# Moving the last-stage chunks of the inverse transform to a block's first step, and holding back one output product in fewer places

## The chip, the cores and the metric

One core of one Trainium2 chip runs the whole program. The time is the device time of one execution in microseconds. Of three timed runs of the kernel before, the median is 2562.79 us (2562.3 to 2563.24). All other times are from one profiled execution, which took 2563.68 us by the same clock; its trace spans 2561.9 us. Instructions stand under their engines: PE (matrix), DVE (vector), ACT (scalar), POOL (GpSimd) and SP, which issues most DMAs.

## What is computed

```
x: (8, 3008, 256)   filt_r, filt_i: (1505, 256)   w_in: (256, 2048)   w_out: (2048, 256)
y = irfft(rfft(x, axis=1) * (filt_r + 1j * filt_i), n=3008, axis=1)
t = y.reshape(24064, 256)
h = t @ w_in
out = (h * clip(h + 3, 0, 6) / 6) @ w_out
```

All of it is in fp32. So there is a circular convolution along the sequence, for eight batches, and behind it a two-layer network with the hardswish function between the layers, for 24064 tokens.

## The kernel before

**Blocks and steps.** The network works on 47 blocks of 512 tokens (256 pairs of tokens). A block has eight steps, one for each 256 of the 2048 hidden features. One pass of the main loop (L1442 on) does the first layer ("up") of step p and the second layer ("down") of the step before it. Both layers are written as seven products of quarter size in place of eight (a Strassen form). The seven up products are in `up_1` (three of them), `up_2` (two), `up_3` and `up_5` (one each); they add up in the two PSUM tiles `al` and `be`. The seven down products are called by number, `down(k, p, 1)` and so on, and add up over the eight steps of a block in four PSUM tiles `po0` to `po3`. In the order of PE, a step without anything special is: up_1, down 1, up_2, down 2 and 4, up_3, down 5 and 6, up_5, down 7 and 3. The down products always belong to the step before.

**What the other engines do in a step.** ACT copies partial sums out of `al` and `be` (L966, L967, L976, L995) and computes the inner clip (`relu`, L1000). DVE adds up the hidden values (L981, L986), multiplies (`hswish`, L1005, twice a step), and makes the sums that the down products need: `g_sums` with L1012 and L1013, and `g_last` with L1018, which product 3 needs. L1005, L1012, L1013 and L1018 read two operands from SBUF; L981, L986 and the output lines read one of theirs from PSUM.

**The turn of a block.** The down products of step 7 of a block run in step 0 of the next. Then the block's result is taken out of `po0` to `po3`: `out_1` (ACT, L1089) behind products 2 and 4 of step 0; `out_2` and `out_3` (DVE, L1098 and L1103) at the end of step 0; `out_4` (DVE, L1107 and L1108, both reading `po2`; POOL, L1109) and `out_5` (DVE, L1112) in step 1. The first product of a new block that writes `po2` is number 5, in step 1. It has to wait until L1108 has read the old value.

**The transform.** While the blocks of one batch run, the transform of the next batches is made in pieces, called from a table `plan`: `plan[step, place]` lists functions, and the loop calls `do(place)` at fixed points of a step. Place 0 is behind `up_1`, place 1 ahead of the first `hswish`, place 2 at the step's end, and places 3 and 4 at its head. The pieces that matter here:

- `n_five` (L881), a last-stage chunk: 40 products of PE (L892, 80 matmul rows in the trace) make 235 pairs of tokens from five rows; ACT copies them to the ring `xn` (L872); when a block's input is complete, `ready` calls `t_sums` (L940): seven POOL additions (L947) that make `xt` from `xn`, both operands from SBUF.
- "Units" (`a8_unit` L608, `b8_unit` L706, `bi8_unit` L779): 16 products in 32 matmul rows that write `al`, `be` and two more PSUM tiles. They stand at place 3, so at the head of a step, ahead of its `up_1`.
- `half_sums`, `a8_folds` (DVE, L522 and L626) and `z8_store` (DMAs from POOL's and SP's queues, L647 and L650): from the second stage to the first of a batch's transform.

Blocks have a kind: for each batch from the third on, the blocks seven to two before its first block are `c a x F F F`; the rest are `t`. `FIVE_AT` (L1311) gives, by kind, the step within a block in which a chunk of five rows is put: three numbers, for a block with one chunk and for the first and second of two. In the kernel before most chunks of `a`, `x` and `F` blocks stand in step 1, place 0.

**Held product.** Where the next step has a unit at its head, the loop leaves product 3 out at the step's end (`held`, L1525) and issues it behind the unit, ahead of products 1 and 2 of the next step, which in such a step also come ahead of `up_1`:

```python
            if units:
                do(3)
                if held:
                    down(*held, 3)
                g_sums(kd, pd)
...
                held = (kd, pd) if (i + 1, 3) in plan and pd < NP - 1 else None
                down(kd, pd, *((7,) if held else (7, 3)))
```

The program has 63 such units, all held.

Of the kernel before, what the change touches and what calls it, by code (L numbers as in the profile page):

```python
# [53 lines left out]
NP = DFF // 256  # L54
# [175 lines left out]
def kernel(  # L230
# [602 lines left out]
    def pair(i):  # L833
        b, js, o, n = chunks[i]
        return b * HC * NA + o, n
# [118 lines left out]
    def product(ps, p, w, x, start=False, stop=False):  # L954
        strips(ps, w_in[p][:, w, :], x, start=start, stop=stop)
# [14 lines left out]
    def up_2(k, p):  # L970
        t = st["xt", k]
        al, be, s, s5 = st["up"]
        h = [hp.tile([P, 512], FP32, name="h%d" % i) for i in range(2)]
        product(al, p, S2, t[:, F3, :])
        product(be[:, 1, :], p, S4, t[:, F5, :], stop=True)
        nc.scalar.activation(out=s[:, 1, :], in_=al, func=AXT.Copy)  # L976
        st["h"] = h
# [10 lines left out]
    def up_4(k, p):  # L988
        st["g", k, p] = gp.tile([P, 7, 256], FP32, name="g")
        relu(0)  # L990
# [46 lines left out]
    def last_down():  # L1037
        p, v, add = NP - 1, nc.vector.tensor_tensor, ALU.add
        g, o = st["g", LAST, p], st["o", LAST][0]
        hswish(LAST, p, 1)  # L1040
        ps = [psF.tile([P, 512], FP32, name="psf", tag="f") for t in range(2)]
        for i, a in ((0, G11), (1, G12)):
            for t in range(2):
                for u in range(2):
                    strips(ps[t][:, ts(u, D)], g[:, a + t, ts(u, P)], w_out[p][:, 2 * i:2 * i + 2, :].rearrange("p j m -> p (j m)"),
                           start=i == 0 and u == 0, stop=i == 1)
        out_4(LAST)
        v(out=o_at(LAST, 0, 1), in0=st["po", LAST][3][:, 1, :, :], in1=o_at(LAST, 0, 1), op=add)
        for t, qs in ((0, (nc.sync, nc.scalar)), (1, (nc.sync, nc.scalar))):
            both = o[:, t, :, :].rearrange("p u d -> p (u d)")  # L1050
            v(out=both, in0=ps[t], in1=both, op=add)
            store_last(t, qs)
# [6 lines left out]
    def plain_up(p):  # L1059
        st["g", 0, p] = gp.tile([P, 7, 256], FP32, name="g")  # L1060
        st["h"] = [psU.tile([P, 512], FP32, name=n) for n in ("al", "be")]
        for i in range(2):
            for d in range(2):
                strips(st["h"][i], w_in[p][:, 2 * d + i, :], xn[:, d, :, 0:PAIRS], start=d == 0, stop=d == 1)
            relu(i)
            hswish(0, p, i)

    def plain_down(p, tokens=(0, 1)):
        g = st["g", 0, p]
        if p == 0:  # L1070
            st["po", 0] = [psO.tile([P, 2, 2, P], FP32, name="po%d" % i) for i in range(2)]
        for t in tokens:
            for u in range(2):
                for i, a in ((0, G11), (1, G12)):
                    strips(st["po", 0][t][:, u, :, :].rearrange("p a m -> p (a m)"), g[:, a + t, ts(u, P)],
                           w_out[p][:, 2 * i:2 * i + 2, :].rearrange("p j m -> p (j m)"),
                           start=p == 0 and u == 0 and i == 0, stop=p == NP - 1)
# [81 lines left out]
    plan = {}  # L1159
# [4 lines left out]
    def at(step, fn, *a):  # L1164
        plan.setdefault((step, 0 if fn in EARLY else 1 if fn is w_scale else 2), []).append((fn, a))

    with tc.manual_schedule():
# [140 lines left out]
                kinds[first[n] - 7 + d] = kind  # L1308

        N_AT = {"c": ((6, 6), (1, 1), (6, 6)), "F": ((0, 0), (1, 1), (6, 6)), "t": ((2, 4), (2, 4), (6, 6))}  # L1310
        FIVE_AT = {"c": (6, 3, 6), "a": (1, 1, 5), "x": (1, 1, 5), "F": (1, 0, 1), "t": (4, 2, 4)}  # L1311
        N_FIRST = {0: ((3, 4),), 1: ((), (2, 2), (3, 3)), 2: ((1, 1),), 3: ((1, 1),)}
        in_block = {}
        for i in range(2, len(chunks)):
# [2 lines left out]
        for i in range(2, len(chunks)):  # L1317
            k = pair(i)[0] // PAIRS
            head = chunks[i][2] == 0
            same = in_block[k]  # L1320
            at_, kind = same.index(i) + 1 if len(same) > 1 else 0, kinds.get(k - 1, "t")
            steps = N_FIRST[k - 1][at_] if k - 1 in N_FIRST else (FIVE_AT[kind][at_],) * 2 if len(chunks[i][1]) == NJ else N_AT[kind][at_]
            if head and len(same) == 1:
                steps = (6, 6)
            s0, s1 = ((k - 1) * NP + s for s in steps)
            five = len(chunks[i][1]) == NJ
            n_at[i] = s1
            if head:
                stored = s0 - 3 + (k == first[1])
            at(max(stored, n_at[i - 2] + 1), t4_load, i)  # L1330
            if five:
                at(s1, n_five, i)
                continue
            at(s0, n_unit, i, 0)
            at(s1, n_unit, i, 1)
# [8 lines left out]
        ZERO_AT = ((6, 1), (6, 1), (7, 0), (7, 1), (8, 0))  # L1344
        ZERO2_AT = ((9, 0), (9, 0), (9, 1), (10, 0), (10, 0))
        A2_AT = (5, 11, 18, 21)
        SUM2_AT = ((0, 1), (3, 4), (10, 14), (15, 16))
        FOLD2_AT = ((7, 8), (12, 13), (19, 20), (22, 23))
        LOAD2_AT = (-4, -2, 5, 11)

        def places(n):
# [23 lines left out]
        for n in range(1, B):  # L1375
# [7 lines left out]
            for c, s in enumerate(a_at):  # L1383
# [7 lines left out]
                k = (first[n] - 7) * NP  # L1391
                sums, folds, load = (SUM2_AT, FOLD2_AT, LOAD2_AT) if n == 2 else (SUM_AT, FOLD_AT, LOAD_AT)
                for d in range(2):
# [46 lines left out]
        held = None  # L1440
        items = [(k, p) for k in range(NBLK) for p in range(NP)]
        for i in range(len(items) + 1):  # L1442
            up = i < len(items)
            k, p = items[min(i, len(items) - 1)]
            dn = i > 0
            kd, pd = items[i - 1]
            def do(place):
                for fn, a in plan.get((i, place), ()):
                    fn(*a)

            if k == 0:
                plain_up(p)
                do(0)
                if dn:
                    plain_down(pd)
                do(1)
                do(2)
                continue
            if not up:
                last_down()  # L1460
                break
            ends = k == LAST and p == NP - 1
            last_plain = dn and kd == 0
            dn = dn and kd > 0
            units = [fn for fn, a in plan.get((i, 3), ())]
            inverse = bool(units)
            ahead = (1, 2) if inverse else (1,) if units else ()
# [5 lines that stand above are left out]
                if not late(i):  # L1473
                    g_last(kd, pd)
                do(4)
                down(kd, pd, *ahead)
                up_1(k, p)
                do(0)
                down(kd, pd, 4 if inverse else 2)
            else:  # L1480
                up_1(k, p)
                do(0)
                if dn:
                    g_sums(kd, pd)
                    if not late(i):
                        g_last(kd, pd)
                    down(kd, pd, 1)
            if up:
                up_2(k, p)
            if dn and pd == 0 and kd > 1:  # L1490
                out_4(kd - 1)
            if up:
                up_2b(k, p)
            if dn:
                down(kd, pd, *((5,) if inverse else (4,) if units else (2, 4)), us=(0,) if inverse else (0, 1))
                if pd == NP - 1:
                    out_1(kd)
            if up:
                up_3(k, p)
                if dn and late(i) and not (pd == 0 and kd > 1):  # L1500
                    g_last(kd, pd)
            if dn:
                down(kd, pd, 5, us=(1,) if inverse else (0, 1))
                down(kd, pd, 6)
            if up:
                up_4(k, p)
            if ends:
                out_1(k)
            if last_plain:
                plain_down(pd, (0,))  # L1510
            if dn and pd == 0 and kd > 1:
                out_5(kd - 1)
                g_last(kd, pd)
            if up:
                do(1)
                hswish(k, p, 0)
            if up:
                up_5(k, p)
            if last_plain:
                plain_down(pd, (1,))  # L1520
                plain_out()
            if dn:
                if pd == NP - 1 or ends:
                    out_2(kd)
                held = (kd, pd) if (i + 1, 3) in plan and pd < NP - 1 else None  # L1525
                down(kd, pd, *((7,) if held else (7, 3)))
                if pd == NP - 1 or ends:
                    out_3(kd)
            do(2)
# [30 lines left out]
```

## Time and profile before

| quantity | value |
|---|---|
| timed runs, median (lowest to highest) | 2562.79 us (2562.3 to 2563.24) |
| profiled execution, its own time | 2563.68 us |
| its span in the trace | 2561.9 us |
| granted PE clock | 1.00 of full speed over the span |
| POOL L947 (`t_sums`), time of one | 727 ns median for `xt<-xn`, 792 ns for `xt<-xt` |
| DVE L1005 (`hswish`), time of one | 746 ns mean of 736 |

How to read it: PE matmuls are pipelined, and a matmul's row lasts until its modelled end, so the rows of successive groups overlap. What counts on PE is the time from the start of one group to the start of the next. The same holds for a step: its length is the time from the first `al<-xt` group of its `up_1` to that of the next step. A row of the timeline is: start in us from the span's start, duration in us, engine, line, operation, output and input tiles, shape, count, and in brackets the idle time before it with what ended it.

### The profile page before, as it was taken

The numbers are of one execution on the slowest core, as the hardware profiler recorded it, in microseconds if no ns is written. First come the engines' busy times: TensorE is split into PE (matmuls) and PEld (weight loads), VectorE is DVE, ScalarE is ACT, GpSimd is POOL, SyncE is SP. The second block draws the span as 40 slices with busy tenths as digits, with TensorE's granted clock in tenths as the row PEclk, the third lists the DMA queues.
The fourth block names the chain that finished last, engine by engine and source line by source line (L and its number), as shares of the span: only waits on it lengthen the run. The fifth ranks groups of instructions, "written<-read, shape, count | busy, mean of one in ns | idle before, by whom it ended". The sixth has DMA issues, their size and how long they took to land.

```text
span 2561.9 us, 87054 instructions
## 1 busy us (share of the span) xinstructions
PE 2542.2 (99%) x37890; PEld 2011.1 (79%) x37890; DVE 2076.5 (81%) x3645; ACT 1321.4 (52%) x2716; POOL 458.7 (18%) x648
## 2 busy tenths in 40 slices
PE   8999999999999999999999999999999999999998
PEld 4488787877888788877887878887788877888887
DVE  6977888888888888888888888888888888766666
ACT  4554455555555555555555555555555555555554
POOL 3252021120211202112021110212102121011110
PEclk9999999999999999999999999999999999999999
DMA  8845545422333133232332323323222232111000
GB/s 234 236 120 164 158 119 153 146 94 86 104 102 115 55 90 110 88 116 59 97 109 80 114 61 105 100 89 105 85 56 63 71 95 71 42 45 26 19 22 26
DMA packets 178180, 245.43 MB, mean 96 GB/s; under 512 B 21354, under 2 KB 143752, under 8 KB 177414
## 3 DMA queue, kind: packets, MB, share of 16 engines
q1 hardware_dynamic: 163997, 200.76, 26.7%
q0 software_dynamic: 13472, 38.81, 5.3%
q8 instruction: 297, 4.87, 0.8%
q14 instruction: 85, 0.70, 0.1%
q10 hardware_dynamic: 329, 0.30, 0.0%
HBM read 164.38 MB, written 128.81 MB: 114 GB/s over the span
## 4 chain that ended last, share of the span: by engine, by line
PE 96%; DVE 1%; DMA 1%; ACT 0%; issue 0%; SPq 0%; DVEq 0%; ACTq 0%
PE po L952 45%; PE al L952 25%; PE be L952 19%; PE psn L892 2%; PE al L779 1%; PE be L608 1%; PE psf L706 1%; DMA bits<-in_moe_w_in_dram 0%; PE psf L693 0%; PE psf L589 0%; ACT h L995 0%; DMA w_all<-in_x_dram 0%; PE psf L763 0%; PE al L608 0%; PE psn L952 0%
## 5 line engine op out<-in xcount | busy, mean ns | idle before, releaser
L952 PEld LDWEIGHTS po<-w_all,g 128*64 128x64 f32 x20808 | 1235.7, 137 | 277.3 <-DVE g L1005 29.4
L952 PE MATMUL po<-w_all,g 128*64 128x128 f32 (+1 forms) x20808 | 1422.6, 275 | 1.9 <-DVE o L1108 1.0
L1000 ACT ACTIVATE r<-h,half_c 128x512 f32<-128x512 f32 x736 | 531.0, 722 | 302.4 <-DVE h L981 290.2
L952 PE MATMUL al<-xt,w_all 128*64 128x256 f32 x4416 | 667.7, 381 | 0.1
L1005 DVE SCALAR_TENSOR_TENSOR g<-r,h 128x512 f32<-128x512 f32 x736 | 546.6, 746 | 95.7 <-ACT r L1000 86.2
L952 PE MATMUL be<-xt,w_all 128*64 128x256 f32 x2944 | 442.9, 379 | 0.0
L981 DVE TENSOR_TENSOR h<-be,s 128x512 f32<-128x512 f32 x368 | 254.1, 690 | 169.1 <-PE be L952 138.2
L995 ACT ACTIVATE h<-al 128x256 f32<-128x256 f32 x368 | 141.0, 383 | 302.1 <-PE al L952 298.1
L952 PEld LDWEIGHTS be<-xt,w_all 128*64 128x64 f32 x2944 | 211.9, 137 | 105.8
L952 PEld LDWEIGHTS al<-xt,w_all 128*64 128x64 f32 x4416 | 275.9, 137 | 6.0 <-POOL w_all L469 1.0
L986 DVE TENSOR_TENSOR h<-al,s 128x256 f32<-128x256 f32 x368 | 156.2, 424 | 150.1 <-PE al L952 150.1
L1013 DVE TENSOR_TENSOR g<-g 128x512 f32<-128x512 f32 x367 | 267.1, 728 | 12.6
L947 POOL TENSOR_TENSOR xt<-xn 128x256 f32<-128x256 f32 x184 | 147.1, 817 | 697.6 <-ACT xn L872 697.6
L952 PE MATMUL al<-xn,w_all 128*64 128x256 f32 (+1 forms) x1536 | 240.1, 392 | 1.0 <-DVE g L1005 0.6
L952 PE MATMUL be<-xn,w_all 128*64 128x256 f32 (+1 forms) x1536 | 236.5, 388 | 0.0
L967 ACT ACTIVATE s<-be 128x256 f32<-128x256 f32 x368 | 141.0, 383 | 176.0 <-PE be L952 176.0
L976 ACT ACTIVATE s<-al 128x256 f32<-128x256 f32 x368 | 141.3, 384 | 160.7 <-PE al L952 160.5
L966 ACT ACTIVATE s<-al 128x256 f32<-128x256 f32 x368 | 141.6, 385 | 102.0 <-PE al L952 102.0
L1012 DVE TENSOR_TENSOR g<-g 128x256 f32<-128x256 f32 x367 | 174.1, 474 | 12.6
L1018 DVE TENSOR_TENSOR g<-g 128x256 f32<-128x256 f32 x367 | 168.0, 458 | 1.5
L796 POOL DMA_DIRECT2D g_tmp<-t x84 | 44.8, 540 | 663.8 <-DVE t L790 663.8
L952 PEld LDWEIGHTS be<-xn,w_all 128*64 128x64 f32 x1536 | 110.5, 137 | 62.0 <-issue 7.4
(192 smaller groups left out, 1887.6 us busy)
## 6 DMA issues: line engine op xcount, KB each, us to landing
g_tmp<-t POOLq DMA_DIRECT2D x96, 256.0 KB, 4.4
x_tmp<-in_x_dram SPq DMA_DIRECT2D x54, 384.0 KB
t<-g_tmp SPq DMA_DIRECT2D x168, 120.0 KB
ft<-f_tmp SPq DMA_DIRECT2D x36, 512.0 KB
t<-zp_tmp SPq DMA_DIRECT2D x36, 512.0 KB
o_tmp<-o SPq DMA_DIRECT2D x46, 256.0 KB
zp_tmp<-y POOLq DMA_DIRECT2D x96, 96.0 KB, 4.3
zp_tmp<-y SPq DMA_DIRECT2D x84, 96.0 KB
```

The costliest lines, as they stand in the source:

```text
L947: nc.gpsimd.tensor_tensor(out=o, in0=x0, in1=x1, op=op_)
L952: nc.tensor.matmul(ps[ds(o, STRIP)], w[:, ds(o, STRIP)], x, skip_group_check=True, **kw)
L966: nc.scalar.activation(out=s[:, 0, :], in_=al, func=AXT.Copy)
L967: nc.scalar.activation(out=s5, in_=be[:, 1, :], func=AXT.Copy)
L976: nc.scalar.activation(out=s[:, 1, :], in_=al, func=AXT.Copy)
L981: nc.vector.tensor_tensor(out=st["h"][0].rearrange("p (a n) -> p a n", a=2), in0=be, in1=s, op=ALU.add)
L986: nc.vector.tensor_tensor(out=st["h"][1][:, 256:512], in0=al, in1=s5, op=ALU.add)
L1000: nc.scalar.activation(out=r, in_=st["h"][i], func=AXT.Relu, bias=half_c, scale=1.0 / 6.0)
L1005: nc.vector.scalar_tensor_tensor(out=st["g", k, p][:, o:o + 2, :].rearrange("p a n -> p (a n)"), in0=st["r", i], scalar=1.0, in1=st["h"][i ...
L1012: v.tensor_tensor(out=g[:, G1, :], in0=g[:, G3, :], in1=g[:, G22, :], op=ALU.add)
L1013: v.tensor_tensor(out=g[:, G3:G2 + 1:2, :], in0=g[:, G3:G1 + 1, :], in1=g[:, G11:G11 + 1, :].broadcast_to([P, 2, 256]), op=ALU.subtract)
L1018: nc.vector.tensor_tensor(out=g[:, G4, :], in0=g[:, G12, :], in1=g[:, G2, :], op=ALU.subtract)
```

## The change

```diff
-        FIVE_AT = {"c": (6, 3, 6), "a": (1, 1, 5), "x": (1, 1, 5), "F": (1, 0, 1), "t": (4, 2, 4)}
+        FIVE_AT = {"c": (6, 3, 6), "a": (0, 0, 5), "x": (1, 1, 5), "F": (0, 0, 1), "t": (4, 2, 4)}
...
-                at(s1, n_five, i)
+                plan.setdefault((s1, 5 if kind in "aF" and at_ < 2 and s1 % NP == 0 else 0), []).append((n_five, (i,)))
...
-        SUM2_AT = ((0, 1), (3, 4), (10, 14), (15, 16))
-        FOLD2_AT = ((7, 8), (12, 13), (19, 20), (22, 23))
+        SUM2_AT = ((0, 1), (3, 4), (10, 12), (15, 16))
+        FOLD2_AT = ((7, 8), (13, 14), (19, 20), (22, 23))
...
             if up:
                 up_2(k, p)
+                do(5)
...
-                held = (kd, pd) if (i + 1, 3) in plan and pd < NP - 1 else None
+                held = (kd, pd) if (i + 1, 3) in plan and any(fn is n_five for fn, a in plan.get((i, 0), ())) else None
```

There are three parts.

1. In blocks of the kinds `a` and `F`, a chunk goes to step 0, at a new place 5 between `up_2` and products 2 and 4. That moves 20 chunks from step 1: one in each of 6 `a` blocks and 14 `F` blocks, each of them followed by a `t_sums`. Two more chunks, in blocks 32 and 37, were in step 0 already, at place 0, and go to place 5; those have no `t_sums`. The DMAs that load a later chunk's input (`t4_load`) are issued one step earlier with them.
2. Product 3 is held back only where the step itself has a chunk at place 0. That leaves 8 of the 63 cases: the `x` blocks and step 1 of blocks 32 and 37.
3. For the third batch, the second pair of `a8_folds` goes from steps 12 and 13 behind that batch's `c` block's start to 13 and 14, and a `half_sums` from 14 to 12.

No instruction is added or taken away.

## Prediction

> **What bounds the kernel now.** First the page's busy times and its chain of what ended last: PE.
>
> ```profile
> span 2561.9 us, 87054 instructions
> PE 2542.2 (99%) x37890; PEld 2011.1 (79%) x37890; DVE 2076.5 (81%) x3645; ACT 1321.4 (52%) x2716; POOL 458.7 (18%) x648
> PE 96%; DVE 1%; DMA 1%; ACT 0%; issue 0%; SPq 0%; DVEq 0%; ACTq 0%
> ```
>
> As no matmul is added or removed, time can only come or go where PE stands still. Those places are few, so the step lengths are next, from the timeline of PE (first `al<-xt` group to first `al<-xt` group). A plain step is 6.08 us. A chunk adds 1.46 (step 0 of block 32: 7.54). A step with a unit behind it is 8.30, and the step after the unit 5.35 (products 1 and 2 went ahead). So a step with a chunk and a unit should be 8.30 + 1.46 = 9.76. The windows of block 27, steps 0 to 2, show 9.95, and those of blocks 33 and 34, steps 0 and 1, show something else:
>
> ```profile
> 1513.17:1519.24 6.07, 6.07 (x88) 5.06 (x86) 5.25 (x10) 3.45 (x8) 2.12 (x4) 1.00 0.57 148
> 1519.24:1529.19 9.95, 9.95 (x217) 7.45 (x214) 8.04 (x14) 5.57 (x11) 5.78 (x7) 1.00 0.06 19
> 1529.19:1534.54 5.35, 5.35 (x72) 4.15 (x70) 5.00 (x9) 2.49 (x6) 0.90 (x2) 1.00 0.25 68
> 1831.69:1838.42 6.73, 6.73 (x104) 5.73 (x102) 5.36 (x9) 4.12 (x12) 5.23 (x9) 1.00 0.58 153
> 1838.42:1847.34 8.92, 8.57 (x137) 6.12 (x135) 8.02 (x16) 4.55 (x9) 3.35 (x4) 1.00 0.14 43
> ```
>
> (Columns: window and length, then busy time of PE, weight loads, DVE, ACT, POOL, with instructions.) Block 33 has no `n_five`, but a short chunk in step 0 with a `t_sums` behind it. Its step 1 should be 8.30 and is 8.92. This is the row the prediction rests on, so here is that stretch on DVE, POOL and PE:
>
> ```profile
> 1836.80 0.76 DVE L1018 TENSOR_TENSOR g<-g 128x256 f32<-128x256 f32 x1
> 1837.48 1.22 DVE L1005 SCALAR_TENSOR_TENSOR g<-r,h 128x512 f32<-128x512 f32 x1
> 1838.62 0.68 DVE L1098 TENSOR_TENSOR o<-po,p 128x512 f32<-128x512 f32 x1
> ...
> 1840.56 0.83 DVE L1012 TENSOR_TENSOR g<-g 128x256 f32<-128x256 f32 x1
> 1841.43 0.69 DVE L1013 TENSOR_TENSOR g<-g 128x512 f32<-128x512 f32 x1
> 1842.04 0.42 DVE L1107 TENSOR_TENSOR o<-po,o 128x256 f32<-128x256 f32 x1
> 1842.37 0.41 DVE L1108 TENSOR_TENSOR o<-po,o 128x256 f32<-128x256 f32 x1
> ```
>
> ```profile
> 1835.15 2.11 POOL L947 TENSOR_TENSOR xt<-xn 128x256 f32<-128x256 f32 x3
> 1837.35 1.95 POOL L947 TENSOR_TENSOR xt<-xt 128x256 f32<-128x256 f32 x2
> 1840.06 1.05 POOL L947 TENSOR_TENSOR xt<-xt 128x256 f32<-128x256 f32 x1
> ```
>
> ```profile
> 1841.89 0.60 PE L952 MATMUL al<-xt,w_all 128*64 128x256 f32 x4
> 1842.84 1.09 PE L952 MATMUL po<-w_all,g 128*64 128x128 f32 x16 [0.35 <-DVE o L1108]
> ```
>
> DVE's additions with two SBUF operands are slow while `t_sums` runs on POOL (L1018 0.76 for 0.41, L1005 1.22 for 0.69, L1012 0.83 for 0.43); those with a PSUM operand are not (L1098 0.68). So L1108 ends 1842.78, and product 5, which writes `po2`, starts 1842.84, where 1841.89 + 0.43 = 1842.32 was due: 0.52 us lost, and 0.10 more in the re-start of the next groups. In block 34, with no chunk, L1108 ends 3.18 us behind the step's start and nothing waits: product 5 is due at 3.90, so DVE has 0.7 us to spare there.
>
> **Part 1, chunks to step 0.** The chunk's own 1.46 us go along unchanged: ahead of it stands `be<-xt` and behind it `po`, as now. What goes: in step 1 of today's 19 such blocks with a unit behind (9.75 to 9.98 us against 9.76), products 1 and 2 wait after the unit for DVE, delayed by `t_sums`; the excess adds up to 3.0 us. Without `t_sums` there, block 33 shows no such wait after its unit. What comes: `t_sums` falls on the turn of the block. Its place follows from rows. In step 0 (plain plan: up_1 1.30, down 1 0.44, up_2 0.86, re-start 0.10) the chunk starts at 2.70. In block 27 `t_sums` starts 2.53 behind the chunk's start (chunk 1520.64, POOL 1523.17). So it starts at 5.23 of a step of 7.54: 2.31 before step 1. In block 33 it started 3.27 before step 1 and ended 2.7 behind it. Everything else in step 0 from product 2 on (p14, L986, relu, L1005, L1098) shifts by the same 1.46 as step 1 does, so DVE's order and dates against step 1 are those of block 33. There `t_sums` caught L1018, the first L1005, a little of the second (0.78) and L1012, and missed L1013. Coming 0.96 later it catches up to all of the second L1005 (1.21, +0.43) and of L1013 (1.10 in block 27, +0.41). The lost time per block is thus between 0.62 (as in block 33) and 0.62 + 0.84 = 1.46. I take half of the extra, **1.04**, as seven additions that last some 6 us from -2.31 end at about 3.7, which catches part of both. For 19 blocks: 19.8 us.
>
> The Trainium skill (SBUF — State Buffer, Who interferes with whom) says that a DVE instruction with two SBUF inputs contends with a GpSimd instruction that reads SBUF, and that the one that comes second is fully blocked till the other ends. The rows agree on which instructions suffer; a wholly overlapped L1005 takes 1.21 and not 0.69 + 0.73.
>
> The 20th block is 5, the third batch's `a` block. There two `a8_folds` (L626, two SBUF operands) stand between L1103 and the second L1005, so L1108 ended 4.39 behind step 1's start even without `t_sums`; only the chunk in step 1 covered that. Uncovered it is 0.5 late; with the 0.8 that L1018 and the first L1005 add, and up to 0.5 each for the two folds and the second L1005, the loss is 1.3 to 2.8. I take 2.6, less the 0.2 lost there now: **+2.4**.
>
> Moves that cost nothing: the `t4_load`s of these chunks were issued at least 17.1 us ahead of their chunk, which now comes some 5 us earlier; the two chunks from place 0 to place 5 have no `t_sums`, and step 0 has no wait. In `a` blocks `z8_store` now stands behind `t_sums` in POOL's queue, some 9 us later, but the next pair of folds that needs its buffer comes over 20 us behind. `out_4`'s POOL addition gets earlier.
>
> **Part 2, holding back.** PE's work between up_5 and product 2 is the same either way; product 3 only changes sides with the unit. 55 cases change. Product 3 needs L1018, which in block 33 ends 1844.37, and product 3 would be due there at 1844.69. The other side: ACT's two copies out of a unit's `al` and `be` end 0.83 and 1.32 behind the unit, and up_1 would write those tiles 0.92 and 1.35 behind it. Nothing, up to 0.02 x 55 = 1.1 us. On the gain side, `bi8_unit` waits for ACT's copy of `al` (waits: 6.0 us of weight loads, 21 times), but its steps are 8.303 us against 8.297 of `a8_unit`, which doesn't wait: 0.1 us in all. **0**.
>
> **Part 3, the folds.** In block 5 the second L626 of the pair stands still for 2.17 us for a store from its buffer, and PE behind it:
>
> ```profile
> 382.82 0.69 DVE L626 TENSOR_TENSOR y<-t 128x512 f32<-128x512 f32 x1
> 385.67 0.69 DVE L626 TENSOR_TENSOR y<-t 128x512 f32<-128x512 f32 x1 [2.17 <-DMA zp_tmp<-y]
> ```
>
> That step is 7.05 us for 6.08. One step later the store is long done, and the `half_sums` (L522, 1.22) that takes its place delays nobody in step 6 of that block, where it stands now: **-0.97**.
>
> **Sum.** 19.8 - 3.0 + 2.4 + 0 - 0.97 = +18.2 us on the profiled execution's 2563.68, so 2581.9; the median is 0.9 below that execution, so **2581.0**, 0.7% slower. Its own range: all blocks at 0.62, block 5 at +1.1: +8.9, so 2571.7; all at 1.46, block 5 at +2.6, and the 1.1 of part 2: 27.7 - 3.0 + 2.6 - 1.0 + 1.1 = +27.4, so 2590.2.
>
> **Rivals.**
> 1. The wait for `po2` does not form. Then only gains are left: -3.0 - 0.2 - 0.97 = -4.2, so 2558.6. It decides at L1108: if it ends by 3.85 of step 1, product 5 is on time. For it speaks the 0.7 us of spare in block 34 and that DVE is idle for 2 us in step 0 during the chunk. Against it: that idle time comes before L986, so it can't be used, and blocks 33 and 39 (8.92, 8.90) both show the wait under an earlier, milder overlap. A partial wait of up to 0.4 a block ends near here too. **Chance 0.11**.
> 2. The held product is what makes `bi8_unit` late: its first matmul comes 0.319 behind the last `po`, against 0.202 for the other units, and if that 0.117 is truly lost, product 3 ahead of the unit saves it 21 times, 2.5 us. On top of rival 1 that is 2556.1, **faster** by 0.26%. It decides at L1108 as 1 does, and by bi8's steps falling below 8.25. Against it: the unit's other matmuls come closer together, so that those steps are as long as a8's. **Chance 0.06**.
> 3. Each SBUF addition of DVE waits for a whole POOL addition (0.73), so that L1018, both L1005, L1012 and L1013 each grow by that. L1108 then ends near 5.9, 2.1 lost a block: 39.9 - 3.0 + 2.6 - 1.0 = +38.5, 2601.3. Read strictly, this is the rule of the page above. The 92 wholly overlapped L1005 rows are against it. **Chance 0.04**.
>
> **How the numbers follow.** The forecast has 0.79. Changes within 0.2% (5.1 us) are what a measurement of this kernel hardly tells from none. Slower: 0.79 + 0.04 = 0.83; same: 0.11; faster: 0.06. The range goes from 2566 (a loss of some 0.3 us a block, below block 33's row) to 2591; left out are the two faster rivals (0.17), and the far end of the third, as near to 2 in 10 as the cases allow.
>
> **What would show it.** In the profile after, step 0 of the `a` and `F` blocks should be 7.54; step 1 8.30 + about 1.0, with the gap between up_3 and product 5 and L1108 as its releaser; L947 rows from 2.3 us before step 1 to 3.7 into it, and the second L1005 and L1013 longer than 0.69. The steps with a unit and no chunk should stay at 8.30. Block 5's step 5 should be 6.08, its step 1 above 8. The prediction is wrong if L1108 ends before 3.9 in those steps, or if up_1 begins to wait for ACT's copies behind the units.

## The result and the profile after

The changed kernel takes 2583.26 us (median of 6 runs, 2582.04 to 2586.59), the kernel before beside it 2562.05 us (6 runs, 2561.29 to 2563.24). The ratio is 1.0085, with a 95% interval of 1.0072 to 1.0098: slower by 0.85%, where 2581.0 us and 0.7% were forecast. The profiled execution took 2582.13 us, at a granted clock of 1.00 as before.

From the page of the kernel after, the span, the busy times and the chain that ended last:

```profile
span 2580.3 us, 87055 instructions
PE 2543.8 (99%) x37890; PEld 1998.2 (77%) x37890; DVE 2067.0 (80%) x3645; ACT 1321.8 (51%) x2716; POOL 463.0 (18%) x648
PE 94%; DVE 4%; issue 1%; ACT 0%; DMA 0%; SPq 0%; DVEq 0%; ACTq 0%
```

DVE's share of the chain goes from 1% to 4%, although DVE is busy for no longer than before: it works as much and is waited for more. The waits of PE say for what (total us, times, longest):

```profile
PE po L952 <- DVE o L1108: 16.3, 23, 1.1
PE po L952 <- DVE g L1005: 3.4, 3, 2.0
```

The first row was 1.0 us in 3 waits before. It is the wait of product 5 for `po2`, at the place where the prediction put it. The windows of steps 0 and 1 of block 27, and of step 1 of block 25, show it by steps (columns as in the prediction):

```profile
1528.45:1535.99 7.54, 7.54 (x168) 6.23 (x166) 5.25 (x10) 4.48 (x10) 4.45 (x7) 1.00 0.52 141
1535.99:1544.98 8.99, 8.45 (x137) 5.93 (x134) 8.09 (x15) 4.13 (x9) 4.93 (x6) 1.00 0.14 39
...
1427.79:1437.36 9.57, 8.46 (x136) 5.86 (x132) 8.67 (x16) 4.10 (x9) 4.45 (x5) 1.00 0.47 147
```

Step 0 is 7.54, as forecast (in four of the 20 moved blocks it is longer, see the last section). Step 1 is not one number. Block 5 apart, it is 8.98 to 9.04 in eight of the 19 blocks, 9.3 to 9.6 in nine, and about 10.1 in blocks 8 and 9. Two of the eight, 17 and 23, belong with the nine by their rows (L1018 takes 0.99 there): their step 0 is 0.57 and 0.62 longer, and the wait in step 1 is shorter by as much. Why there are two lengths is in the rows of DVE and POOL. First block 27, DVE and then POOL:

```profile
1534.37 0.42 DVE L1018 TENSOR_TENSOR g<-g 128x256 f32<-128x256 f32 x1
1534.89 1.02 DVE L1005 SCALAR_TENSOR_TENSOR g<-r,h 128x512 f32<-128x512 f32 x1
...
1536.96 0.91 DVE L1005 SCALAR_TENSOR_TENSOR g<-r,h 128x512 f32<-128x512 f32 x1
1537.90 0.84 DVE L1012 TENSOR_TENSOR g<-g 128x256 f32<-128x256 f32 x1
1538.78 1.10 DVE L1013 TENSOR_TENSOR g<-g 128x512 f32<-128x512 f32 x1
...
1540.13 0.41 DVE L1108 TENSOR_TENSOR o<-po,o 128x256 f32<-128x256 f32 x1
```

```profile
1533.67 2.84 POOL L947 TENSOR_TENSOR xt<-xn 128x256 f32<-128x256 f32 x3 [1.77 <-ACT xn L872]
...
1539.41 1.05 POOL L947 TENSOR_TENSOR xt<-xt 128x256 f32<-128x256 f32 x1
```

And block 25, DVE and POOL:

```profile
1426.17 0.98 DVE L1018 TENSOR_TENSOR g<-g 128x256 f32<-128x256 f32 x1
1427.08 1.22 DVE L1005 SCALAR_TENSOR_TENSOR g<-r,h 128x512 f32<-128x512 f32 x1
...
1432.51 0.41 DVE L1108 TENSOR_TENSOR o<-po,o 128x256 f32<-128x256 f32 x1
```

```profile
1425.46 2.28 POOL L947 TENSOR_TENSOR xt<-xn 128x256 f32<-128x256 f32 x3 [2.96 <-ACT xn L872]
```

`t_sums` starts 2.32 us ahead of step 1 in both (1535.99 - 1533.67), where 2.31 was forecast. DVE's L1018 and the second of POOL's seven additions then start within 0.02 us of one another in both. In block 27 DVE comes first: L1018 takes its 0.42, and POOL's first three additions take 2.84. In block 25 POOL comes first: L1018 takes 0.98, the first L1005 behind it 1.22 instead of 1.02, and the three additions only 2.28. From the second L1005 on, both blocks are alike. L1108 ends 4.55 into step 1 in the one and 5.13 in the other; product 5 was due at 3.90. The rows of PE at those places, block 27 and then block 25:

```profile
1539.45 0.60 PE L952 MATMUL al<-xt,w_all 128*64 128x256 f32 x4
1540.60 1.09 PE L952 MATMUL po<-w_all,g 128*64 128x128 f32 x16 [0.54 <-DVE o L1108]
```

```profile
1432.97 1.09 PE L952 MATMUL po<-w_all,g 128*64 128x128 f32 x16 [1.11 <-DVE o L1108]
```

(From start to start, 1539.45 to 1540.60 is 1.15 us for 0.43: 0.72 lost.)

### The profile page after: what moved, and what is told of

Its sections match the earlier page's. It is cut to its first block, busy times and chain, and to the rows that moved or that the text cites. A ratio compares the mean times of both kernels' runs of the same rounds, so it can differ in the third digit from the quotient of the medians.

```text
span 2580.3 us, 87055 instructions
## 1 busy us (share of the span) xinstructions
PE 2543.8 (99%) x37890; PEld 1998.2 (77%) x37890; DVE 2067.0 (80%) x3645; ACT 1321.8 (51%) x2716; POOL 463.0 (18%) x648
## 4 chain that ended last, share of the span: by engine, by line
PE 94%; DVE 4%; issue 1%; ACT 0%; DMA 0%; SPq 0%; DVEq 0%; ACTq 0%
PE po L952 44%; PE al L952 24%; PE be L952 18%; PE psn L892 2%; DVE g L1005 1%; PE be L608 1%; PE al L779 1%; DVE g L1012 1%; PE psf L706 1%; PE psf L693 0%; DVE o L1107 0%; DVE o L1103 0%; PE psf L763 0%; DVE o L1098 0%; PE psf L589 0%
## 5 line engine op out<-in xcount | busy, mean ns | idle before, releaser
L1005 DVE SCALAR_TENSOR_TENSOR g<-r,h 128x512 f32<-128x512 f32 x736 | 541.8, 737 | 105.5 <-ACT r L1000 97.0
L986 DVE TENSOR_TENSOR h<-al,s 128x256 f32<-128x256 f32 x368 | 155.9, 424 | 172.2 <-PE al L952 172.1
L1013 DVE TENSOR_TENSOR g<-g 128x512 f32<-128x512 f32 x367 | 265.8, 724 | 12.6
L947 POOL TENSOR_TENSOR xt<-xn 128x256 f32<-128x256 f32 x184 | 153.2, 852 | 643.4 <-ACT xn L872 643.3
L1012 DVE TENSOR_TENSOR g<-g 128x256 f32<-128x256 f32 x367 | 174.0, 474 | 12.6
L1018 DVE TENSOR_TENSOR g<-g 128x256 f32<-128x256 f32 x367 | 166.9, 455 | 1.5
```

The source lines that it names most:

```text
L947: nc.gpsimd.tensor_tensor(out=o, in0=x0, in1=x1, op=op_)
L986: nc.vector.tensor_tensor(out=st["h"][1][:, 256:512], in0=al, in1=s5, op=ALU.add)
L1005: nc.vector.scalar_tensor_tensor(out=st["g", k, p][:, o:o + 2, :].rearrange("p a n -> p (a n)"), in0=st["r", i], scalar=1.0, in1=st["h"][i ...
L1012: v.tensor_tensor(out=g[:, G1, :], in0=g[:, G3, :], in1=g[:, G22, :], op=ALU.add)
L1013: v.tensor_tensor(out=g[:, G3:G2 + 1:2, :], in0=g[:, G3:G1 + 1, :], in1=g[:, G11:G11 + 1, :].broadcast_to([P, 2, 256]), op=ALU.subtract)
L1018: nc.vector.tensor_tensor(out=g[:, G4, :], in0=g[:, G12, :], in1=g[:, G2, :], op=ALU.subtract)
```

## The experiments

Each kernel was timed against the kernel before in five rounds. Differences "by the steps" are sums of the step lengths in one profiled execution, against those of before; by this measure the changed kernel stands at +18.6 us. Where a kernel adds lines, the lines in its profile move by two or three: L1008 is then L1005, and L1111 is L1108.

### The three parts, each by itself

Part 1 alone:

```diff
-                at(s1, n_five, i)
+                plan.setdefault((s1, 5 if kind in "aF" and at_ < 2 and s1 % NP == 0 else 0), []).append((n_five, (i,)))
```

(with the `FIVE_AT` of the change and `do(5)` behind `up_2`)

> The kernel before with part 1 alone: the chunks of the a and F blocks in step 0, place 5; product 3 held as before, folds as before. Theory (t_sums on POOL falls on the turn of the block, DVE gets slow there, L1108 is late and product 5 waits): all of the loss is here. The profile after lost 18.6 us net although the steps with a unit outside the moved blocks gained about 0.09 each and block 5's fold 0.97; taking those back, +22 to +25 us against before. Rival (the loss comes from product 3 no longer being held): nearly no loss, within 5 us of before.

Measured: 2586.78 us, ratio 1.0094 (1.008 to 1.0108), +23.7 us by the steps. Moved blocks lose about 0.62 or 1.22 us each (block 5 loses 2.7, blocks 8 and 9 lose 1.8), the unit steps stay at 8.30. Blocks 20 and 26 have changed places against the kernel after (9.10 and 9.70, there 9.60 and 9.01), with the same instructions around the turn: the length isn't a property of the block. All of the loss is in part 1.

Part 2 alone:

```diff
-                held = (kd, pd) if (i + 1, 3) in plan and pd < NP - 1 else None
+                held = (kd, pd) if (i + 1, 3) in plan and any(fn is n_five for fn, a in plan.get((i, 0), ())) else None
```

> The kernel before with part 2 alone: product 3 held only behind a chunk at place 0 of the same step, which here still includes step 1 of the a and F blocks; so some 33 units lose their held product. The prediction on record said 0. The profile after says -0.08 to -0.09 a unit and -0.43 in each of blocks 2 and 3: -3 to -4 us. The rival that blames the held product for the loss says slower by several us.

Measured: 2558.71 us, ratio 0.9986 (0.9977 to 0.9995), -4.0 us by the steps. It is a gain and was forecast as nothing. A unit step goes from 8.30 to 8.17, the step behind it from 5.35 to 5.39. Here is the head of one `a8_unit` before, PE and ACT:

```profile
634.19 0.61 PE L608 MATMUL be<-t,wa 24*32 24x512 f32 x1
634.31 0.61 PE L608 MATMUL al<-t,wa 24*32 24x512 f32 x1
```

```profile
633.87 0.38 ACT L995 ACTIVATE h<-al 128x256 f32<-128x256 f32 x1 [1.09 <-PE al L952]
```

And the same unit with part 2:

```profile
633.10 0.61 PE L608 MATMUL be<-t,wa 24*32 24x512 f32 x1
633.11 0.61 PE L608 MATMUL al<-t,wa 24*32 24x512 f32 x1
```

Before, the unit's first write to `al` comes 0.12 behind its first write to `be`, 0.05 to 0.06 behind the end of ACT's copy of the old `al` (633.87 + 0.38 = 634.25). It is so in all 63 units before the change, whichever of the three kinds: the first write to `al` comes 0.05 behind that copy. With product 3 ahead of the unit the copy is long done, and the gap is 0.01. Of the 4.0 us some 2.5 come from steps of this kind; step 2 of blocks 2 and 3 gives 0.43 each, step 5 of block 5 0.38 (see part 3), and what sets the size in blocks 2 and 3 was not followed. The other side shows in the weight loads of PE, with part 2:

```profile
PEld be L952 <- ACT t L783: 5.4, 21, 0.3
```

That row is new, and so are those for L612 and L712, the same copies behind the other two kinds of unit: `up_1` now waits for the unit's `be` to be copied out, and this gives back 0.04 a unit.

Part 3 alone:

```diff
-        SUM2_AT = ((0, 1), (3, 4), (10, 14), (15, 16))
-        FOLD2_AT = ((7, 8), (12, 13), (19, 20), (22, 23))
+        SUM2_AT = ((0, 1), (3, 4), (10, 12), (15, 16))
+        FOLD2_AT = ((7, 8), (13, 14), (19, 20), (22, 23))
```

> The kernel before with part 3 alone. Both theories: -0.97 us, as predicted, all of it in step 5 of block 5 (7.05 to 6.08).

Measured: 2562.56 us, ratio 1.0 (0.9991 to 1.0009). In the steps it is -1.0, and block 5's step 5 goes from 7.05 to 6.08; the timing can't tell so little. By the steps the three parts come to 23.7 - 4.0 - 1.0 = 18.7, with 18.6 for all together. That they add up so well is in part chance: step 5 of block 5 gets shorter in all three kernels, by 0.72 with part 1, 0.38 with part 2 and 0.97 with part 3, and it can be shortened by 0.97 only once.

### The chunk without the overlap

The chunk stays in step 0, but its `t_sums` is issued behind `out_4` in step 1:

```diff
-            t_sums(t // PAIRS)
+            if later:
+                st["due"] = t // PAIRS
+            else:
+                t_sums(t // PAIRS)
...
                 out_4(kd - 1)
+                if "due" in st:
+                    t_sums(st.pop("due"))
```

> The changed kernel with one thing moved: the seven additions of t_sums of the moved chunks are issued behind out_4 of step 1 in POOL's order, so they start some 4 us into step 1 and not 2.3 us ahead of it. The chunk, its copies on ACT and its missing cover in step 1 stay as in the changed kernel. Theory: L1108 is on time (3.2 us into step 1), product 5 doesn't wait, and only the gains of parts 2 and 3 are left, with the old 0.17 a block back behind the unit: 2556 to 2559 us, 5 us or so below before. Rival 1 (it is the chunk's cover that step 1 lacks, or ACT's copies ahead of out_1 that make the turn late): the wait stays, 2580 or more.

Measured: 2556.73 us, ratio 0.9977 (0.9968 to 0.9987), -4.9 us by the steps: faster than the kernel before. DVE at the turn of block 27 (step 1 starts at 1516.51), and then POOL:

```profile
1514.89 0.41 DVE L1021 TENSOR_TENSOR g<-g 128x256 f32<-128x256 f32 x1
1515.42 0.69 DVE L1008 SCALAR_TENSOR_TENSOR g<-r,h 128x512 f32<-128x512 f32 x1
...
1517.15 0.68 DVE L1008 SCALAR_TENSOR_TENSOR g<-r,h 128x512 f32<-128x512 f32 x1
...
1518.33 0.69 DVE L1016 TENSOR_TENSOR g<-g 128x512 f32<-128x512 f32 x1
...
1519.28 0.41 DVE L1111 TENSOR_TENSOR o<-po,o 128x256 f32<-128x256 f32 x1
```

```profile
1520.20 2.29 POOL L950 TENSOR_TENSOR xt<-xn 128x256 f32<-128x256 f32 x3
```

All rows shown have their free durations, L1111 ends 3.18 into the step, as in block 34 before, and the step is 8.21. So the wait comes from the overlap with `t_sums` alone. That the turn has lost its cover (the chunk's 1.46 us of PE work in step 1) costs nothing by itself, but for block 5, where the two folds stand in DVE's order: there product 5 starts 0.49 late, as the prediction had it (0.5), and step 1 is 6.78.

### Moving the overlap in time

Three kernels change how much of `t_sums` meets the turn. Chunk at place 0 of step 0, so that `t_sums` starts 1.3 us earlier:

```diff
-                plan.setdefault((s1, 5 if kind in "aF" and at_ < 2 and s1 % NP == 0 else 0), []).append((n_five, (i,)))
+                plan.setdefault((s1, 0), []).append((n_five, (i,)))
```

> The changed kernel with the moved chunks at place 0 of step 0 (behind up_1, ahead of product 1) and not at place 5. The chunk and its missing cover in step 1 are the same, but t_sums starts some 1.3 us earlier, 3.6 us ahead of step 1. Theory (what matters is how much of t_sums falls on step 1's additions): the wait for product 5 falls from 0.95 a block to about 0.5, block 33's value: 2570 to 2576. Rival (missing cover, whatever t_sums does): no change from 2583.

Measured: 2563.45 us, ratio 1.0007 (0.9998 to 1.0016). The direction is as expected, the size much larger: step 1 is 8.46 in most blocks. Block 27, DVE:

```profile
1521.63 0.78 DVE L1005 SCALAR_TENSOR_TENSOR g<-r,h 128x512 f32<-128x512 f32 x1
1522.45 0.83 DVE L1012 TENSOR_TENSOR g<-g 128x256 f32<-128x256 f32 x1
1523.32 0.69 DVE L1013 TENSOR_TENSOR g<-g 128x512 f32<-128x512 f32 x1
```

L1013 is free here and the second L1005 almost.

`g_last` (L1018) issued right behind `g_sums` in those steps, so that it is out of the way of `t_sums`:

```diff
         def late(i):
+            if (i, 5) in plan:
+                return False
```

> The changed kernel with step 0's g_last (L1018) issued right behind g_sums in the steps with a moved chunk, so that it is done before t_sums starts. One addition fewer overlaps, and the next L1005 starts when its relu is ready. Theory: all blocks have the shorter of the two waits seen in the changed kernel (0.70 and not 1.28) or less: 5 to 9 us less than 2583, so 2574 to 2578. If the date of L1018 doesn't matter, 2583.

Measured: 2571.26 us, ratio 1.0035 (1.0022 to 1.0047), somewhat better than expected. Step 1 is 8.67 to 8.78 in 13 of the 19 blocks, among them blocks of both lengths. Block 27, DVE:

```profile
1521.99 0.43 DVE L1018 TENSOR_TENSOR g<-g 128x256 f32<-128x256 f32 x1
...
1525.58 0.75 DVE L1005 SCALAR_TENSOR_TENSOR g<-r,h 128x512 f32<-128x512 f32 x1 [0.44 <-ACT r L1000]
```

L1018 now runs 2 us ahead of `t_sums`, at 0.43, and the first L1005 grows by only 0.06; the second L1005, L1012 and L1013 are as in the kernel after (0.90, 0.83, 1.10).

A POOL subtraction of 16 columns (its result is overwritten) ahead of `t_sums` of the moved chunks, to let DVE always come first:

```diff
+        if tiny:
+            nc.gpsimd.tensor_tensor(out=f1[:, 240:256], in0=c0[:, 240:256], in1=s0[:, 240:256], op=ALU.subtract)
```

> The changed kernel with one more POOL addition, of 16 columns, ahead of t_sums of the moved chunks (it computes columns that the next addition writes again), so that POOL's second large addition comes a little later. In the changed kernel that one and DVE's L1018 start within 20 ns of each other: where L1018 is first it takes 0.42 and the block waits 0.70; where POOL is first L1018 takes 0.98 and the block waits 1.28. If the order decides, delaying POOL makes the program faster: nearly all blocks at about 0.7, some 5 us below 2583. If the two waits have another cause, no change or slower by the added addition.

Measured: 2580.52 us, ratio 1.0069 (1.0056 to 1.0083). One length in place of two, about 9.2 in most blocks, but it lies between the two and not at the shorter. Block 25, POOL and then DVE:

```profile
1423.57 0.23 POOL L946 TENSOR_TENSOR xt<-xn 128x16 f32<-128x16 f32 x1 [2.94 <-ACT xn L872]
1423.87 2.75 POOL L949 TENSOR_TENSOR xt<-xn 128x256 f32<-128x256 f32 x3
```

```profile
1424.28 0.60 DVE L1020 TENSOR_TENSOR g<-g 128x256 f32<-128x256 f32 x1
1424.81 1.21 DVE L1007 SCALAR_TENSOR_TENSOR g<-r,h 128x512 f32<-128x512 f32 x1
```

With the delay of 0.30 L1018 meets the end of POOL's first addition (0.60), and L1005 is wholly overlapped (1.21). A shift of 0.3 us changes which rows suffer, so the order alone does not set the price.

These kernels give one account. Add what the five SBUF operations of DVE grew by (of L1018 only what goes beyond 0.10, as DVE is idle for that long behind it, waiting for the `relu`), take away the 0.7 of spare read from block 34, and what is left is the wait:

| kernel, block | L1018 | 1st L1005 | 2nd L1005 | L1012 | L1013 | growth | less 0.7 | measured wait |
|---|---|---|---|---|---|---|---|---|
| after, 27 | 0.42 | 1.02 | 0.91 | 0.84 | 1.10 | 1.38 | 0.68 | 0.71 |
| after, 25 | 0.98 | 1.22 | 0.90 | 0.84 | 1.10 | 2.04 | 1.34 | 1.29 |
| chunk at place 0, 27 | 0.41 | 1.02 | 0.78 | 0.83 | 0.69 | 0.83 | 0.13 | 0.17 |
| early `g_last`, 27 | away | 0.75 | 0.90 | 0.83 | 1.10 | 1.09 | 0.39 | 0.43 |
| small subtraction, 25 | 0.60 | 1.21 | 0.91 | 0.84 | 1.10 | 1.66 | 0.96 | 0.92 |
| `t_sums` in step 1, 27 | 0.41 | 0.69 | 0.68 | 0.42 | 0.69 | 0 | none | none |

(Free: 0.41, 0.69, 0.69, 0.42, 0.69. Measured: step 1 less 8.17, less 0.11 for the re-start of the two groups behind the wait.) The same sum gives the wait of product 5, read from its start, to within 0.08 in 66 of 68 moved blocks of the kernels of rows 1, 3, 4 and 5 and of part 1 alone; left out are blocks 5, 8 and 9, where DVE has more in its order, and those with a lengthened first step (last section).

### How far the better version goes

`x` blocks treated in the same way as in the kernel without the overlap:

```diff
-"x": (1, 1, 5)
+"x": (0, 1, 5)
-                mid = kind in "aF" and at_ < 2 and s1 % NP == 0
+                mid = kind in "axF" and at_ < 2 and s1 % NP == 0
```

> As e4 (t_sums behind out_4), and the chunks of the six x blocks go the same way: step 0, place 5, no held product there. Theory: the x blocks lose their wait behind the unit (9.93 + 5.35 against 7.54 + 8.20 + 5.39 - 6.08, some 0.2 each), so 1 to 1.5 us below e4, 2555 to 2556. If the chunk in step 0 costs by itself, slower than e4.

Measured: 2561.31 us, ratio 0.9996 (0.9987 to 1.0005): the gain is gone. DVE at the turn of block 24, an `x` block (step 1 starts at 1359.51), and PE's row of product 5:

```profile
1360.16 1.22 DVE L522 TENSOR_TENSOR xs<-xs,wa 128x1024 f32<-128x1024 f32 x1
1361.29 0.69 DVE L1008 SCALAR_TENSOR_TENSOR g<-r,h 128x512 f32<-128x512 f32 x1
```

```profile
1363.88 1.09 PE L955 MATMUL po<-w_all,g 128*64 128x128 f32 x16 [0.30 <-DVE o L1111]
```

In `x` blocks a `half_sums` of 1.22 us stands at the turn. It is more than the 0.7 of spare; the difference of 0.52 should be the wait, and 0.47 is measured (8.75 less 8.17, less 0.11). Here the chunk in step 1 had been the cover. I had not looked at what else is queued at that turn. Block 18 loses 1.16 more in step 0, of which the last section tells.

Parts 2 and 3 together without part 1, to see what the place of the chunk is worth:

```diff
-                plan.setdefault((s1, 5 if kind in "aF" and at_ < 2 and s1 % NP == 0 else 0), []).append((n_five, (i,)))
+                at(s1, n_five, i)
```

(with the `FIVE_AT` of before, and without `do(5)`)

> Parts 2 and 3 without part 1. If the parts add up (part 2 alone was 4.0 us and part 3 alone 1.0 us in the profile), this is 5.0 us below the kernel before, so about 2557.5, with steps of units at 8.17 and block 5's step 5 at 6.08 and nothing else changed. Set beside the kernel with all three parts and t_sums behind out_4 (4.9 us below in the profile) this tells what the place of the chunk is worth by itself. Theory: nothing to speak of, the two are within 0.5 us of one another in the profile, as the 2 to 3 us that the chunk's old place cost behind the unit are spent again in blocks 5 and 7 and in lengthened first steps. Rival: the chunk's new place brings the 3.0 us of the prediction, hidden so far by something else, and this kernel is then 2 to 3 us slower than that one.

Measured: 2558.63 us, ratio 0.9985 (0.9976 to 0.9994), -4.4 us by the steps. That is 0.6 short of the sum of the two parts, as part 2 alone had already taken 0.4 from block 5's step 5. It is half a microsecond from the -4.9 with the chunks in step 0. So at place 5 the move of the chunk is worth next to nothing even without its harm.

The last kernel has the late `t_sums` and the chunks at place 0:

```diff
-                plan.setdefault((s1, 5 if mid else 0), []).append((n_five, (i, mid)))
+                plan.setdefault((s1, 0), []).append((n_five, (i, mid)))
```

> All three parts with t_sums behind out_4, but the moved chunks at place 0 of step 0, behind up_1, in place of place 5. The wait for product 5 should be as absent as with place 5 (step 1 of the moved blocks 8.2). Theory: the lengthened first steps of single blocks (0.1 to 0.6 us in 8, 11, 17 and 23) belong to place 5, where two products of 8 matmul rows follow the chunk; at place 0 all first steps are then 7.54 or 7.62, and the profile is 0.5 to 1.3 us below that of place 5, so 5.4 to 6.2 us below the kernel before, median 2556 to 2557. Rival: they belong to any chunk of 80 short matmuls in step 0 that meets a transfer of the instruction queue; then some first steps are 0.2 us or more longer here too and the profile is where it was, 4.9 below.

Measured: 2555.53 us, ratio 0.9973 (0.9963 to 0.9983), -6.2 us by the steps, the fastest of all. The first steps are 7.54 to 7.67 in all moved blocks. Against the kernel at place 5 its interval overlaps; by the steps it is 1.3 us ahead, 0.7 of it in the first steps (0.8 to the good in blocks 8, 11, 17 and 23, 0.2 to the bad in 29 and 35). Part of the rest is a delay in a unit's matmuls that hits block 7 there (0.9) and block 25 here (0.6); its cause was not followed. Against parts 2 and 3 without part 1 it is 1.8 us ahead by the steps: the 19 blocks are 2.3 us shorter, which is about what the chunk's old place had cost, and block 5 is 0.5 longer. The wait for product 5 is close to where it was before the change (1.0 us in 3 waits):

```profile
PE po L955 <- DVE o L1111: 1.4, 4, 0.4
```

## Why the prediction was right, point by point

- **Part 1, the wait for `po2`: right, and it makes the result.** Forecast for 19 blocks 19.8 us. In the kernel after, the waits for L1108 in those blocks, from start to start, add up to 18.4, and the re-starts behind them, 0.11 each, to 2.1: 20.5. The start of `t_sums` was right to 0.01 in most blocks. The kernel with the late `t_sums` shows that the overlap is the cause.
- **How the 1.04 a block came about: wrong, and right as a mean only.** I took block 33's loss and half of what L1013 and the second L1005 could add. But those two grew in nearly every block (1.10 and 0.91), and the rows in which the blocks differ are L1018 and the first L1005, which I had taken as settled by block 33. There are two lengths, some 0.8 and 1.4 with the re-start, and hardly a block at 1.04; the mean is 1.08. The range of 0.62 to 1.46 held both. `t_sums` ends 4.47 into step 1 of block 27 and 3.91 into that of block 25, not at 3.7, because the overlap slows POOL too (in block 27 its third addition takes 1.18 and not 0.73).
- **Block 5: right.** Forecast +2.4; steps 0 to 3 give 1.46 + 1.27 - 0.12 + 0.04 = +2.65. The wait is mostly product 2's, for the second L1005 behind the folds (the longest, 2.0, in the second row of PE's waits above), and not product 5's.
- **The waits of the old place, -3.0: could not be seen apart.** Block by block the new length is the sum of both. Without the overlap and with the chunks at place 0, 2.3 us of it show; at place 5 most of that is spent again in block 7 and in lengthened first steps.
- **Part 2, costed at 0: the step that failed.** I set `bi8_unit`'s wait of 0.117 aside because its steps are as long as those of "`a8_unit`, which doesn't wait". `a8_unit` does wait, on its second matmul instead of its first, and so gives no measure. Part 2 alone brings -4.0 us. Rival 2 had the mechanism, for 21 of the 55 units, and its mark (steps below 8.25) came true; but it was tied to rival 1, which did not. So the unit steps did not stay at 8.30, as was expected. And `up_1` did begin to wait for ACT's copies behind the units, which the prediction had named as a sign that it is wrong: the spare of 0.03 was not enough, at a cost of 0.04 a unit.
- **Part 3: right.** -0.97 forecast and seen.
- **Not foreseen.** In blocks 8 and 9 the third batch's `table_sign` (L369) stands in DVE's order between L1103 and the second L1005, as the folds do in block 5. It costs a second wait, 0.82 and 0.89. Block 8, DVE and then PE:

```profile
519.15 1.32 DVE L369 TENSOR_SCALAR ft<-ft,wa 128x256 f32<-128x256 f32 x2
520.39 1.21 DVE L1005 SCALAR_TENSOR_TENSOR g<-r,h 128x512 f32<-128x512 f32 x1
```

```profile
521.66 1.09 PE L952 MATMUL po<-w_all,g 128*64 128x128 f32 x16 [0.61 <-DVE g L1005]
```

And some first steps were lengthened (below), 1.6 us in all. Nearly all of it came back: blocks 11, 17 and 23 lose 1.17 to 1.19 over steps 0 to 3, like the other blocks with the longer wait (1.18 to 1.25), as DVE goes on while PE stands still.

So the forecast of +18.2 for a measured +18.6 owes something to luck. The main term was right. But over steps 0 to 3 the 19 blocks lose 20.5 net, where 19.8 - 3.0 = 16.8 was forecast, and part 2 gives 3.6 outside those steps, where nothing was forecast: two errors of nearly one size, with opposite signs.

- **The rivals.** 1 (no wait) and 3 (each SBUF addition of DVE waits for a whole POOL addition) did not happen. For 3, the Trainium skill (SBUF — State Buffer, Who interferes with whom) adds that the order of issue, not the operation, decides who is blocked. The two lengths agree with that: L1018 took 0.42 or 0.98 by who came first, with starts at most 0.02 us apart. But a chain of additions behind it settles to L1005 at 1.22, not 0.69 + 0.73 = 1.42. Two numbers of rival 3 were wrong in themselves: the rows of L1005 that last 1.15 or more before the change are 77, not 92, and five operations that each grow by 0.73 put L1108 near 6.6, not 5.9. Nothing else hangs on either.

## What to carry to other kernels

Before work is moved, list what the other engines have queued at the place it goes to, and where the spare at that place is: here 0.7 us of DVE before L1108 decided nearly every block, and the wait was the growth of five operations less that 0.7. A transfer of work that looks free on the bounding engine may bring a follower on another engine (`t_sums` on POOL) that meets operations there; sending the follower later by itself turned +0.85% into -0.23% (parts 2 and 3 by themselves give -0.15%). And a reference that "doesn't wait" must be looked at as closely as the row that it is to judge.

## What the runs showed that I had not expected

**Two lengths from one program.** Blocks in which POOL's second addition starts just ahead of L1018 are 0.6 us longer than those in which it starts just behind, mostly with starts within 0.02 us of one another, and the blocks concerned change from one kernel to the next. In the 20 moved blocks of the kernel after, L1018 takes 0.41 or 0.42 in the eight where it starts at most 0.002 behind that addition, and 0.83 to 1.01 in the twelve where it starts 0.005 or more behind. Where it starts 0.07, 0.13 and 0.17 behind (blocks 19, 13, 7) it takes 0.95, 0.88 and 0.83, so that it always ends about 1.0 behind the addition's start. With part 1 alone the two groups overlap by some 0.01, which is as finely as these starts can be told apart. That the order of these two is the cause is read from the rows; the kernel that was to force the order moved the overlap as well.

**A stall of PE without a releaser.** Block 23's step 0 in the kernel after is 8.16 for 7.54, with this on PE:

```profile
1319.53 0.61 PE L952 MATMUL po<-w_all,g 128*64 128x128 f32 x8
1320.53 0.66 PE L952 MATMUL po<-w_all,g 128*64 128x128 f32 x8 [0.40 <-DVE h L986]
```

Product 6, in the last row, needs nothing from L986. In the kernel with the `x` blocks the page puts the same down to "issue", and it is longest there:

```profile
1038.29 0.76 PE L955 MATMUL po<-w_all,g 128*64 128x128 f32 x9
1040.00 0.55 PE L955 MATMUL po<-w_all,g 128*64 128x128 f32 x6 [0.95 <-issue]
```

It comes only behind a chunk at place 5, whose 80 matmuls with their weight loads pass in 1.31 us, and in blocks that change in part from kernel to kernel: block 23 has it in all six kernels with chunks at place 5, blocks 8 and 17 in five, the others in fewer. In these six, 26 first steps are longer than 7.59, and in 25 of them a transfer on the instruction queue (q8) ends 1.6 to 2.45 us behind the chunk's start. So it does in 25 of the 112 others, and they are not longer. At place 0 no such transfer ends at those dates, and first steps are 7.54 or, in five blocks, 7.60 to 7.67. That points to PE's supply with instructions, but a coincidence of dates is no proof, and 25 cases speak against its being enough; the cause stays open. The Trainium skill (Runtime: NRT & Kernel Launch, Instruction fetch mechanics) says that instructions come in blocks of 16 KiB and that crossing into a new one is mostly hidden; whether these 0.06 to 1.16 us are cases where it isn't, no run here settles.
